# Moving the product with v beside the next tile's scores in a hand-planned attention and two-MLP kernel on one Trainium2 core

## Chip, cores and metric

One core of one Trainium2 chip. The metric is device time in microseconds (us) of one execution, from the launch of the program to its end; the kernel before takes 927.84 us (median of three runs).

## What is computed

Attention over 4 batches, 8 heads, 576 positions and head size 64, causal with a window of 128 and an ALiBi bias; then two MLPs over the resulting 2304 x 512 matrix. Cut to what matters:

```python
scores = scale * q @ k.T                     # per batch and head
scores = where(0 <= rel < 128, scores - slope * |rel|, -1e9)
attn = exp(scores - max) / (sum + 1e-9)
x = (attn @ v) as (2304, 512)
x = (silu(x @ w_gate) * (x @ w_val)) @ w_out        # d_ff 1536
out = silu(x @ w_in) @ w_out2                       # d_ff 2048
```

Everything is float32. Large products are made from a high and a low float32r part in three passes.

## The kernel before

The 2304 tokens are 18 tiles of 128 (tile 0 to tile 17), in three parts of six (`PT = 6`). Part by part the MLPs run over the 768 tokens of a part: `moe1` with 6 groups, `moe2` with 8. While they run over one part, the attention of the next part is worked in between, tile by tile. In this document part one is tiles 0 to 5, part two tiles 6 to 11, part three tiles 12 to 17.

No loop of the kernel runs in the order in which it is written. Every operation is handed to `plan.add` with an engine (or two to choose from), a cost in ns, a due time, the keys that it reads and writes, and the PSUM banks that it takes and gives back. `Plan.issue` (L95) then plays the engines forward: each time it takes the engine that can start earliest, and on it the operation that can start now and has the earliest due time (equal due times go in the order of `add`). The due time is no gate. An engine that has nothing else starts whatever is ready, so on the planner's idle engines (ScalarE, SyncE's DMA queue) things go as soon as they are ready; TensorE nearly always has a choice, and there the due time decides. The result is one fixed order for each engine; on the chip each engine works through its own order and waits on semaphores.

The eight PSUM banks are dealt out by the planner too (L341): at most 6 for the MLP products (`mm`), at most 6 for attention (`att`, of which 4 for scores `S`, 1 for the product with v `O`, 2 for turned probabilities `C`, 1 for transposes `T`), at most 4 for operand differences (`B`).

The attention of a tile i from tile 6 on (L1266 to L1278), both halves of four heads together:

- `load` (L406): k, q and v of the tile, by SyncE's queue (L425). v has a ring of three buffers, so the load of v for tile i + 3 has to wait for the products that read tile i.
- `prepare` (L433): TensorE transposes k (L445) and q (L453); copies and differences on ScalarE and VectorE.
- `score` (L473, matmuls L493): 24 matmuls in TensorE tiles of 64 x 128, four banks at once, due at(i).
- `attend` (L503): masks (L520) and bias (L527) on VectorE, exponent (L533) on ScalarE, normalisation on VectorE and GpSimd (L549, L550, L553), turning on TensorE (L570), copy to `u` on ScalarE, and two selections on GpSimd (L577 to `l`, L584 to `u`). They are due at(i), at(i + 1/4), at(i + 1/2) and at(i + 3/4). `u` has three buffers, `l` two.
- `weigh` (L590, matmuls L607): the product with v, 32 matmuls in TensorE tiles of 128 x 64, one bank, and one copy of 512 columns to `XST` (a `copy_op`, L348 on ScalarE). It was due at(i + 3/4), the time of the last turns of its own tile.

`at` is a line in each part: 33 us of due time a tile for tiles 6, 7, 8 and again for 9, 10, 11, with a leap between (at(9) is 132.96 us of due time after at(6)); about 39.1 us a tile in part three. Tiles 0 to 5 go by halves.

`operands` (L674) makes the Strassen operands of a part from `XST` or `ACC`, with up to four `B` banks. `out_sums` (L859) in part three loads kept output weights (`word`, `top`, L868), adds them (L357 on VectorE or L358 on GpSimd) and stores sums.

Of the kernel before, what the change touches and what calls it, by code (L numbers as in the profile page):

```python
# [201 lines left out]
def attention_moe_moe2_kernel(  # L202
# [40 lines left out]
    PT = NT // P // 3  # L243
    BT = PT // 2
    N = BT * P
    NP = H // 2
    G1, G2 = F1 // (2 * P), F2 // (2 * P)
    EARLY = 6
# [94 lines left out]
    def cost(kind, n):  # L343
        a, b = COST[kind]
        return a + b * n

    def copy_op(n, due, out, src, reads, writes, give=None, psum=True, slack=0.0):
        act = lambda: nc.scalar.activation(out(), src(), AF.Copy)  # L348
        dve = lambda: nc.vector.tensor_copy(out(), src())  # L349
        plan.add(  # L350
            "act", cost("act_ps" if psum else "act", n), due, act, reads, writes, give=give,
            other=[("dve", cost("dve", n), dve, not psum, 500.0)], slack=slack,
        )
# [46 lines left out]
    def first(i):  # L400
        return (i * P) % S == 0
# [4 lines left out]
    def load(i, nm, due):  # L406
        src, dst, slot = {
            "k": (k, KLD_R, i % 2),
            "q": (q, QLD_R, i % 2),
            "v": (v, VLD_R, i % 3),  # L410
        }[nm]
        t = dst[slot]
        step = H // 2 if i == 0 else H
        for h0 in range(0, H, step):
            for off, n, b, s in runs(i * P, P):
                o = t[off:off + n, h0:h0 + step]
                a = src[b, h0:h0 + step, s:s + n, :].rearrange("h s d -> s h d")
                keys = [
                    (nm, slot, hf, r)
                    for hf in range(2) if h0 <= 4 * hf < h0 + step  # L420
                    for r in range(2) if off <= 64 * r < off + n
                ]
                plan.add(
                    "sp", 1460.0 * step * n / (H * P), due,
                    lambda o=o, a=a: nc.sync.dma_start(out=o, in_=a),  # L425
                    writes=keys,
                )

    def loaded(i, nm, hf):
        slot = i % (3 if nm == "v" else 2)  # L430
        return [(nm, slot, hf, r) for r in range(2)]

    def prepare(i, hf, due):  # L433
        kn, qn = KLD_R[i % 2], QLD_R[i % 2]
        kr = KR[:, :, 2 * hf:2 * hf + 2, i % 2, :]
        bk, bq = Bank("T"), Bank("T")
        pk = lambda: bk.tile.rearrange("p (a b) -> p a b", b=P)
        pq = lambda: bq.tile.rearrange("p (a b) -> p a b", b=P)
        slot = (2 * i + hf) % len(QT_R)
        qt = QT_R[slot]  # L440

        def k_turn():
            for j in range(2):
                h = 4 * hf + 2 * j
                nc.tensor.transpose(pk()[:, j, :], kn[:, h:h + 2].rearrange("p h d -> p (h d)"), ident)  # L445

        def k_lo():
            nc.vector.tensor_tensor(kr[:, 1], pk()[:, 0:2], kr[:, 0].bitcast(F32), ALU.subtract)

        def q_turn():  # L450
            for j in range(2):
                h = 4 * hf + 2 * j
                nc.tensor.transpose(pq()[:, j, :], qn[:, h:h + 2].rearrange("p h d -> p (h d)"), ident)  # L453

        def q_hi():
            nc.scalar.activation(qt[:, 0], pq()[:, 0:2], AF.Copy, scale=-0.125)

        def q_lo():
            nc.vector.scalar_tensor_tensor(
                qt[:, 1], pq()[:, 0:2], -0.125, qt[:, 0].bitcast(F32), ALU.mult, ALU.subtract  # L460
            )

        kk, qk = ("KR", i % 2, hf), ("qt", slot)
        plan.add("pe", 2 * 109, due, k_turn, loaded(i, "k", hf) + ["ident"], [bk], take=bk)
        copy_op(256, due, lambda: kr[:, 0], lambda: pk()[:, 0:2], [bk], [kk])
        plan.add("dve", cost("dve", 256), due, k_lo, [bk, kk], [kk], give=bk)
        plan.add("pe", 2 * 109, due, q_turn, loaded(i, "q", hf) + ["ident"], [bq], take=bq)
        plan.add("act", cost("act_ps", 256), due, q_hi, [bq], [qk])
        plan.add("dve", cost("dve", 256), due, q_lo, [bq], [qk], give=bq)
# [120 lines left out]
    def weigh(i, halves, due):  # L590

        ob = Bank("O")
        ops = lambda hf: ob.tile.rearrange("p (a b) -> p a b", b=P)[:, 2 * hf:2 * hf + 2]
        parts, reads = {}, []
        for hf in halves:
            us, ls = (2 * i + hf) % len(U_R), (2 * i + hf) % len(L_R)
            parts[hf] = [(i, U_R[us])] if first(i) else [(i - 1, U_R[us]), (i, L_R[ls])]
            reads += [("uu", us)] + ([] if first(i) else [("l", ls)])
            reads += [x for tl, _ in parts[hf] for x in loaded(tl, "v", hf)]

        def product():
            for hf in halves:
                for p in range(2):
                    for a, (tl, m) in enumerate(parts[hf]):
                        for j in range(2):
                            l = 2 * p + j
                            nc.tensor.matmul(  # L607
                                ops(hf)[64 * j:64 * j + 64, p, :],
                                VLD_R[tl % len(VLD_R)][:, 4 * hf + l, :],
                                m[:, l, :],  # L610
                                start=(a == 0),
                                stop=(a == len(parts[hf]) - 1),
                            )

        plan.add("pe", 218 * len(halves) * (1 if first(i) else 2) + 290, due, product, reads, [ob], take=ob)
        ti = i % PT
        for n, hf in enumerate(halves):
            last = hf == halves[-1]
            xk = [("xt", ti, 2 * hf + p) for p in range(2)]
            if i >= PT:  # L620
                if last and len(halves) == 2:
                    all_k = [("xt", ti, c) for c in range(KC)]
                    copy_op(
                        512, due, lambda: XST[:, ti], lambda: ob.tile.rearrange("p (a b) -> p a b", b=P), [ob], all_k, give=ob
                    )
                elif len(halves) == 1:
                    copy_op(256, due, lambda: XST[:, ti, 2 * hf:2 * hf + 2], lambda: ops(hf), [ob], xk, give=ob)
                continue
            slot, t0 = x_slot(hf, ti // BT), (ti % BT) * P
            xh, xl = XOP[:, slot, 0, :, t0:t0 + P], XOP[:, slot, 1, :, t0:t0 + P]  # L630
            keys = [("X", slot, kk, ti % BT) for kk in range(2)]
            copy_op(256, due, lambda xh=xh, hf=hf: xh, lambda hf=hf: ops(hf), [ob], keys)
            plan.add(
                "dve", cost("dve", 256), due,
                lambda xl=xl, xh=xh, hf=hf: nc.vector.tensor_tensor(xl, ops(hf), xh.bitcast(F32), ALU.subtract),
                [ob] + [("ob", i, h) for h in halves[:n]], keys + [("ob", i, hf)], give=ob if last else None,
            )


    def x_slot(j, b):  # L640

        return ((0, 1), (2, 3))[j][b]
# [623 lines left out]
    def attention_part(part, at):  # L1266
        for i in range(part * PT, part * PT + PT):
            load(i, "k", at(i) - 14820.0)
            load(i, "q", at(i) - 20070.0)
            load(i, "v", at(i) - 7670.0)  # L1270
            for halves in [(0,), (1,)] if i < EARLY else [(0, 1)]:
                t0 = at(i + 0.5 * halves[0])
                for hf in halves:
                    prepare(i, hf, t0 - 8000.0)
                banks = score(i, halves, t0)
                for hf in halves:
                    attend(i, hf, [at(i + p / NP) for p in (2 * hf, 2 * hf + 1)], banks[hf])
                weigh(i, halves, at(i + 0.5 * halves[-1] + 1 / NP))  # L1278

    def ramp(x):  # L1280
        return 5000.0 + 6130.0 * min(x, 1) + 10170.0 * min(max(x - 1, 0), 1) + 7700.0 * max(x - 2, 0)
# [93 lines left out]
    def spread(part, t0, span):  # L1375
        attention_part(part, lambda x: t0 + (x - part * PT) / PT * span)

    attention_part(0, ramp)
    moe1_plain([0])
    t_next = state["t"] + 6000.0  # L1380
# [4 lines left out]
    t_moe2 = t_next - 6000.0 + (G1 - GP) * 22 * pe_cost(6, N) + (GP - 1) * 24 * pe_cost(6, N)  # L1385
    early = lambda x: t_next + 0.0 + (x - PT) * 33000.0
    attention_part(1, lambda x: early(x) if x < PT + PT // 2 else t_moe2 + 20000.0 + (x - PT - PT // 2) * 33000.0)
    moe1(0, range(GP, G1), "raw", True)
    flush()
# [52 lines left out]
```

## Time and profile before

| what | us |
| --- | --- |
| median of 3 runs | 927.84 (926.32 to 929.77) |
| the profiled execution | 929.85 |
| its span, first to last instruction | 928.1 |
| TensorE busy in the span | 907.4 (98%), 5758 matmuls |
| VectorE, ScalarE, GpSimd busy | 670.2, 531.3, 539.6 |

Read the engine shares first, then the stretches: the attention of parts two and three lies between about 114 and 640 us. In the timeline a row is one run of like instructions: start, duration, engine, line, what is written and read, the TensorE tile, the shape and the count; in square brackets how long the engine sat idle before it and who ended that. Durations of matmuls overlap, so the distance from start to start tells what one costs.

### The profile page before, as it was taken

How to read it: one execution, taken by the hardware profiler on the slowest of the kernel's cores; microseconds unless marked ns; L12 is line 12 of the kernel's file. 1: busy time of each engine (PE TensorE's matmuls, PEld its weight loads, DVE VectorE, ACT ScalarE, POOL GpSimd, SP SyncE). 2: the span in 40 equal slices, each digit the busy share in tenths (PEclk: the TensorE clock that was granted, in tenths of full speed). 3: DMA queues.
4: the chain of work that ended last, by engine and by line, in shares of the span. 5: the costliest groups of instructions: out<-in, count | busy, mean ns of one | idle time of the engine just before them, and what ended most of it. 6: DMA issues, size and time to landing. Idle time of an engine off the chain costs nothing.

```text
span 928.1 us, 17773 instructions
## 1 busy us (share of the span) xinstructions
PE 907.4 (98%) x5758; PEld 844.4 (91%) x5758; DVE 670.2 (72%) x1554; ACT 531.3 (57%) x1361; POOL 539.6 (58%) x628
## 2 busy tenths in 40 slices
PE   7999999999999999999999999999999999999998
PEld 5889899998987888999999889889899999999997
DVE  7888869889979788747576877676734666736663
ACT  6887567667967685754343575544354333474531
POOL 2766377787546669674331555464333335788566
PEclk9999999999999999999999999999999999999999
DMA  9988896898888987999877787978898888587702
GB/s 225 271 238 275 253 331 208 286 322 286 267 263 273 292 298 264 346 317 302 273 259 236 253 280 263 334 278 288 292 307 251 252 252 251 187 257 247 220 24 91
DMA packets 181676, 241.57 MB, mean 260 GB/s; under 512 B 68048, under 2 KB 97232, under 8 KB 181584
## 3 DMA queue, kind: packets, MB, share of 16 engines
q1 hardware_dynamic: 181584, 240.44, 79.8%
q8 instruction: 46, 0.75, 0.3%
q14 instruction: 46, 0.38, 0.1%
HBM read 169.61 MB, written 70.78 MB: 259 GB/s over the span
## 4 chain that ended last, share of the span: by engine, by line
PE 78%; DVE 10%; DMA 5%; POOL 2%; ACT 2%; issue 2%; SPq 0%; DVEq 0%; ACTq 0%; POOLq 0%
PE bank L905 15%; PE bank L906 14%; PE bank L907 14%; PE bank L1234 5%; PE bank L1236 4%; PE bank L1235 4%; PE bank L493 3%; PE bank L607 3%; PE bank L1201 3%; PE bank L1203 3%; PE bank L1202 3%; DMA raw<-in_moe_w_in_dram 2%; DVE word L758 2%; PE bank L1132 2%; PE bank L1131 2%
## 5 line engine op out<-in xcount | busy, mean ns | idle before, releaser
L905 PE MATMUL bank<-XOP,wu 128*128 128x384 f32 (+1 forms) x868 | 296.7, 342 | 6.9 <-DVE tmp L349 1.9
L906 PE MATMUL bank<-XOP,wu 128*128 128x384 f32 (+1 forms) x868 | 289.3, 333 | 1.7 <-DVE XOP L357 1.0
L907 PE MATMUL bank<-XOP,wu 128*128 128x384 f32 (+1 forms) x868 | 288.9, 333 | 0.0
L905 PEld LDWEIGHTS bank<-XOP,wu 128*128 128x128 f32 x868 | 163.1, 188 | 16.8 <-ACT tmp L348 3.3
L906 PEld LDWEIGHTS bank<-XOP,wu 128*128 128x128 f32 x868 | 163.4, 188 | 4.5 <-DVE XOP L357 2.4
L907 PEld LDWEIGHTS bank<-XOP,wu 128*128 128x128 f32 x868 | 163.1, 188 | 0.1
L348 ACT ACTIVATE tmp<-bank 128x384 f32<-128x384 f32 x133 | 62.2, 489 | 67.7 <-PE bank L907 45.3
L358 POOL TENSOR_TENSOR h<-tmp,h 128x384 fp32r<-128x384 f32 x55 | 56.6, 1037 | 72.2 <-ACT h L348 72.1
L1234 PE MATMUL bank<-wo,h 128*128 128x512 f32 (+1 forms) x218 | 87.2, 400 | 0.1
L1236 PE MATMUL bank<-wo,h 128*128 128x512 f32 (+1 forms) x218 | 85.6, 393 | 0.0
L1235 PE MATMUL bank<-wo,h 128*128 128x512 f32 (+1 forms) x218 | 85.6, 392 | 0.0
L1246 DVE TENSOR_TENSOR ACC<-bank,ACC 128x512 f32<-128x512 f32 (+1 forms) x97 | 64.2, 679 | 21.6 <-PE bank L1236 15.5
L951 DVE TENSOR_TENSOR bank<-bank,tmp 128x384 f32<-128x384 f32 x93 | 52.3, 562 | 32.9 <-PE bank L907 27.9
L358 POOL TENSOR_TENSOR wu<-word,wu 128x256 fp32r<-128x256 f32 x63 | 50.1, 809 | 44.5 <-ACT wu L348 39.3
L553 POOL TENSOR_TENSOR cs<-cs,st 128x512 f32<-128x512 f32 x36 | 39.5, 1097 | 62.5 <-DVE st L550 45.8
L1201 PE MATMUL bank<-h,wo 128*128 128x384 f32 (+1 forms) x216 | 72.9, 338 | 0.1
L1203 PE MATMUL bank<-h,wo 128*128 128x384 f32 (+1 forms) x216 | 71.4, 331 | 0.0
L1202 PE MATMUL bank<-h,wo 128*128 128x384 f32 (+1 forms) x216 | 71.4, 330 | 0.0
L758 DVE SCALAR_TENSOR_TENSOR word<-raw,top 128x512 int32<-128x512 int32 x68 | 59.2, 871 | 11.0 <-ACT top L755 9.0
L533 ACT ACTIVATE cs<-cs,st 128x128 f32<-128x128 f32 x144 | 56.2, 394 | 15.0 <-DVE st L527 14.8
L755 ACT ACTIVATE top<-raw 128x512 f16<-128x512 bf16 x68 | 53.7, 790 | 17.9 <-DMA raw<-in_moe_w_in_dram 6.4
L358 POOL TENSOR_TENSOR wu<-sums,wu 128x256 fp32r<-128x256 f32 x78 | 61.5, 818 | 0.9 <-ACT wu L348 0.9
(417 smaller groups left out, 2116.5 us busy)
## 6 DMA issues: line engine op xcount, KB each, us to landing
wu<-kept_i SPq DMA_DIRECT2D x112, 256.0 KB, 3.4
wu<-kept_g SPq DMA_DIRECT2D x72, 256.0 KB, 4.2
wu<-kept_v SPq DMA_DIRECT2D x72, 256.0 KB, 4.1
wo<-kept_o SPq DMA_DIRECT2D x34, 512.0 KB, 4.5
raw<-in_moe_w_out_dram SPq DMA_DIRECT2D x28, 512.0 KB, 4.7
kept_o<-wo SPq DMA_DIRECT2D x28, 512.0 KB, 4.2
kept_i<-wu SPq DMA_DIRECT2D x56, 256.0 KB, 3.3
kept_s<-later_raw SPq DMA_DIRECT2D x44, 256.0 KB, 4.4
```

Source lines behind the costliest of these rows:

```text
L358: pool = lambda: nc.gpsimd.tensor_tensor(out(), x(), y(), op)
L758: lambda: nc.vector.scalar_tensor_tensor(w.bitcast(I32), word, 13, top, ALU.logical_shift_right, ALU.bitwise_or),
L905: nc.tensor.matmul(ps, wh, xh, start=start, stop=False, skip_group_check=True)
L906: nc.tensor.matmul(ps, wh, xl, start=False, stop=False, skip_group_check=True)
L907: nc.tensor.matmul(ps, wl, xh, start=False, stop=stop, skip_group_check=True)
L1201: nc.tensor.matmul(ps[:, 0:n], wh, h[:, 0], start=(i == 0), stop=False)
L1202: nc.tensor.matmul(ps[:, 0:n], wh, h[:, 1], start=False, stop=False)
L1203: nc.tensor.matmul(ps[:, 0:n], wl, h[:, 0], start=False, stop=(i == 1))
L1234: nc.tensor.matmul(ps, hh, wh, start=(i == 0), stop=False)
L1235: nc.tensor.matmul(ps, hh, wl, start=False, stop=False)
L1236: nc.tensor.matmul(ps, hl, wh, start=False, stop=(i == 1))
L1246: plan.add("dve", cost("dve", n), due, lambda: nc.vector.tensor_tensor(acc, pv(), acc, ALU.add), [b], keys, give=b)
```

## The change

`weigh` of a tile from tile 6 on, if it isn't the last of its part, is due at(i + 1) in place of at(i + 3/4). at(i + 1) is also the due time of the scores of tile i + 1. Nothing else changes: no operation is added or left out. `EARLY` is 6, so this meets tiles 6 to 10 and 12 to 16; tiles 11 and 17 keep their due time, and so do tiles 0 to 5.

```diff
@@ -1275,7 +1275,8 @@
                 banks = score(i, halves, t0)
                 for hf in halves:
                     attend(i, hf, [at(i + p / NP) for p in (2 * hf, 2 * hf + 1)], banks[hf])
-                weigh(i, halves, at(i + 0.5 * halves[-1] + 1 / NP))
+                paired = i >= EARLY and i + 1 < part * PT + PT
+                weigh(i, halves, at(i + 1) if paired else at(i + 0.5 * halves[-1] + 1 / NP))
```

## Rows read from the trace of the kernel before

**Rows 1.** The page: busy time of each engine, share of the span, instructions

```profile
PE 907.4 (98%) x5758; PEld 844.4 (91%) x5758; DVE 670.2 (72%) x1554; ACT 531.3 (57%) x1361; POOL 539.6 (58%) x628
```

**Rows 2.** A stretch: length, busy time by engine, granted clock, DMA share, GB/s

```profile
114.00:640.00 526.00, 518.45 (x3210) 477.56 (x3212) 406.88 (x922) 325.95 (x838) 318.06 (x390) 1.00 0.85 284
```

**Rows 3.** PE timeline: moved products with v of tiles 9 and 16, scores after

```profile
270.10 1.09 PE L607 MATMUL bank<-u,vld 128*64 128x128 f32 x16
...
280.23 1.68 PE L493 MATMUL bank<-KR,qts 64*128 64x256 f32 x24
...
593.68 0.44 PE L607 MATMUL bank<-u,vld 128*64 128x128 f32 x4
...
595.02 0.44 PE L607 MATMUL bank<-u,vld 128*64 128x128 f32 x4 [0.24 <-POOL u L584]
...
603.88 1.64 PE L493 MATMUL bank<-KR,qts 64*128 64x256 f32 x24
```

**Rows 4.** PE timeline: scores of tile 8 in the main stream

```profile
160.95 0.34 PE L907 MATMUL bank<-XOP,wu 128*128 128x384 f32 x1
161.22 1.63 PE L493 MATMUL bank<-KR,qts 64*128 64x256 f32 x24
```

**Rows 5.** PE timeline: tile 7's product with v, its end and the passes after

```profile
163.50 0.44 PE L607 MATMUL bank<-u,vld 128*64 128x128 f32 x4
...
165.08 0.39 PE L607 MATMUL bank<-l,vld 128*64 128x128 f32 x4
165.40 0.45 PE L905 MATMUL bank<-XOP,wu 128*128 128x384 f32 x1
165.68 0.34 PE L906 MATMUL bank<-XOP,wu 128*128 128x384 f32 x1
165.86 0.33 PE L907 MATMUL bank<-XOP,wu 128*128 128x384 f32 x1
```

**Rows 6.** PE timeline, part one: scores right behind a product with v

```profile
33.00 0.39 PE L607 MATMUL bank<-u,vld 128*64 128x128 f32 x4
33.22 0.39 PE L607 MATMUL bank<-l,vld 128*64 128x128 f32 x4
33.53 0.97 PE L493 MATMUL bank<-KR,qts 64*128 64x256 f32 x12
```

**Rows 7.** PE timeline: end of tile 10's product with v, transposes behind it

```profile
313.36 0.39 PE L607 MATMUL bank<-l,vld 128*64 128x128 f32 x4
313.68 0.44 PE L445 MATMUL bank<-ident,klds 128*128 128x128 f32 x2
```

**Rows 8.** PE timeline: tile 6's product with v, scores of tile 7

```profile
117.06 0.44 PE L607 MATMUL bank<-u,vld 128*64 128x128 f32 x4
...
137.53 1.65 PE L493 MATMUL bank<-KR,qts 64*128 64x256 f32 x24
```

**Rows 9.** PE, DVE and SP timelines: a stall between tile 12's product and tile 13's scores

```profile
410.75 0.44 PE L607 MATMUL bank<-u,vld 128*64 128x128 f32 x4
...
417.34 0.44 PE L905 MATMUL bank<-XOP,wu 128*128 128x384 f32 x1 [0.64 <-ACT tmp L348]
...
415.20 0.69 DVE L357 TENSOR_TENSOR word<-word,top 128x512 f32<-128x512 f32 x1 [3.47 <-DMA wu<-kept_g]
...
407.56 0.32 SPq L868 DMA_DIRECT2D word<-kept_o  x1
```

**Rows 10.** Transfers that write word, 404 to 418 us: issue to landing

```profile
DMA to landing us min/median/max: 7.5/7.5/7.5
```

**Rows 11.** SyncE's queue waiting for the product with v: us in total, times, longest

```profile
SPq L425 <- PE bank L607: 13.6, 5, 4.6
```

**Rows 12.** DVE timeline: a mask behind the scores of tile 15

```profile
511.59 0.43 DVE L520 COPY_PREDICATED bank<-m_up,bank 128x256 f32<-128x256 uint8 x1 [1.93 <-PE bank L493]
```

**Rows 13.** PE timeline: the longest stall after the scores of tile 10

```profile
291.02 0.44 PE L905 MATMUL bank<-XOP,wu 128*128 128x384 f32 x1 [1.93 <-DVE tmp L349]
```

**Rows 14.** DVE timeline: a transfer awaited behind tile 14's product with v

```profile
503.25 0.69 DVE L357 TENSOR_TENSOR word<-word,top 128x512 f32<-128x512 f32 x1 [2.27 <-DMA top<-kept_o]
```

## Prediction

> **What bounds the kernel now.** The page's busy shares come first: TensorE is busy for 98% of the span, VectorE for 72% and the others for less than 60% [rows 1]. So the end is set by how much TensorE has to do and by how long it stands. The change touches only tiles 6 to 16, so I next cut out the stretch from 114 to 640 us: TensorE is busy for 518.45 of 526.00 us at a granted clock of 1.00 [rows 2], its upper level of 2.4 GHz. The clock has nothing to give back, and the whole visible idle time there is 526.00 - 518.45 = 7.55 us. No change of order in this stretch can win more than that 7.55 us and what TensorE loses inside its busy time when it passes from one kind of matmul to another. The timeline, read from start to start, shows those losses; it is the third view. The fourth is the queues of VectorE and SyncE at the places where TensorE stands.
>
> **What moves.** Nothing is added or removed. Ten products with v (tiles 6 to 10, 12 to 16) get a later due time, 8.25 us of due time for tiles 6, 7, 9 and 10, a quarter of 39.1, or 9.8, for 12 to 16, and 42 for tile 8, whose next tile starts after the leap in `at`. On TensorE the due time decides, so each product should be issued where the scores of the next tile are issued now, and just ahead of them, as it was added first. For tile 9 that is from 270.10 to about 280, for tile 16 from 593.68 to about 603 [rows 3]; these and tiles 10, 12, 13, 14 and 15 make seven that I expect to pair, with distances of about 8 to 11 us. The MLP stream between the two places comes 1.9 us earlier (one product takes 165.40 - 163.50 us [rows 5]), and from the scores on everything stands where it stood. So the sum has small terms only.
>
> **Passing from one kind of matmul to another.** Passes of the main stream start 0.18 us apart (165.68, 165.86) [rows 5], matmuls of the product 0.22 us a group of four (33.00, 33.22) [rows 6].
> - Into the scores from the main stream: 161.22 - 160.95 = 0.27, so 0.09 over [rows 4].
> - Out of the product: 165.40 - 165.08 = 0.32, so 0.10 over; then the first pass takes 165.68 - 165.40 = 0.28, again 0.10 over [rows 5].
> - From the product straight into scores: part one has it, 33.53 - 33.22 = 0.31, so 0.09 over [rows 6].
>
> A pair therefore keeps the last of these and loses the exit of the product (0.10 + 0.10) while the entry into the scores is the one it keeps: 0.20 saved. That holds for tile 9. For the other six, transposes stand right behind the product now, at 0.32 in place of 0.22 [rows 7]; they share its way back to the main stream, and will have a slow first pass of their own afterwards. There only the one boundary of 0.10 goes. Sum: 0.20 + 6 x 0.10 = 0.8 us saved. Bounds: nothing, if no pair forms, and 10 x 0.20 = 2.0 us, if all do and the transposes find other company.
>
> The Trainium skill ("TensorEngine Tiling (Array Packing)", Tiling Modes, Key Properties) says that a change of the tiling mode drains TensorE. It speaks against part of the gain, as the product (128 x 64) and the scores (64 x 128) are different modes and a pair still changes in between; the 0.09 of rows 6 agrees. By that rule alone a pair saves one change of four, 7 x 0.1 = 0.7 us, about the same as the sum has.
>
> Why seven and not ten: the scores take four banks at once, and behind a product that has just taken one they need a fifth. One row speaks for five being there: tile 7's product ran 2.3 us after the scores of tile 8 [rows 4, 5], with one group of passes between. That tile is as good as adjacent now, and waits for its own inputs; I expect no change. Tile 6's scores come 20.5 us after its product [rows 8], twice the distance of the others for 8.25 us of due time: they were held by banks (operand differences take up to four there), not by the due time, so the product will go before them, not with them. Tile 8's product lands in the scores of tile 9, where the first output products of a new MLP stage run beside its input products; I count no pair.
>
> **The wait of tile 16's product.** It stood 0.24 us for the last selection on GpSimd [rows 3]. Some 10 us later its inputs are long there: 0.2 us saved.
>
> **The stall behind tile 12.** Between the old place (410.75) and the scores of tile 13, TensorE stands for 0.64 us at 417.34, for a copy that hangs on VectorE; VectorE had stood for 3.47 us at 415.20 for a loaded `word` [rows 9]. That load was issued at 407.56 [rows 9] and took 7.5 us [rows 10], so it lands at 415.06, and it was issued ahead of the product that moves. With the product gone from 410.75, TensorE reaches the same place 1.9 us earlier and stands 1.9 us longer: the time that the product used to cover is lost here. That is the upper end, +1.9. The lower end is -0.6: with the product moved the planner may put VectorE's addition for the main stream ahead of the sum of `word`, and the stall goes. The order of two operations decides it; the transfer speaks for the upper end, the planner's freedom for the lower. I take +0.6, near the middle, and keep both ends.
>
> **What else is moved, and costed at nothing.** Each moved product draws a copy to `XST` behind it on ScalarE, busy for 326 of 526 us [rows 2]; if it held up main-stream copies by its 0.6 us or so each time and TensorE waited, the seven would cost about 4 us. The load of v three tiles on goes out when the product is done. SyncE's queue stands for it now, 13.6 us in five waits, the longest 4.6 [rows 11], with the weight loads queued behind; these waits move to the scores, and the v is wanted more than a tile later. VectorE's masks now wait for the scores by up to 1.93 us [rows 12] with the main-stream evacuations queued behind. The planner counts a product at 1.16 us (4 x 218 + 290 ns) while it takes 1.9, so each pair can make this wait 0.74 longer, 7 x 0.74 = 5.2 us if all of it reached TensorE. I take zero, since none of it does behind the row of 511.59: TensorE runs its queue on. `u` and `l` are held some 10 us longer, but the next tile writes its first `l` only after its scores.
>
> **The sum.** -0.8 - 0.2 + 0.6 = -0.4 us. The profiled execution took 929.85 us (928.1 span and 1.75 around it), 2.0 above the median; by the sum it becomes 929.4, and the median 927.84 becomes 927.4. A measurement of this kernel can tell about 0.5% (4.64 us) from no change: below 923.2 is faster, above 932.5 slower. My forecast is no change.
>
> **Rivals.**
> - *No pairs* (the change does not do what it says): the product goes first, takes a bank, and the scores wait for their four until the copy to `XST` is done, with main-stream passes between. Then nothing is saved at the boundaries, and the stall costs its upper end: -0.2 + 1.9 = +1.7, 929.5. For it: four banks at once, six for the main stream. Against: the fifth bank of rows 4 and 5.
> - *Slower*: the early main stream runs into transfers that have their own time. In each gap between old and new place it comes 1.9 us early, and where VectorE's queue stands for a load the 1.9 is lost, as behind tile 12. It decides from four of the seven gaps on: 4 x 1.9 - 1.0 = +6.6, 934.4. For it: DMA is busy 85% of the stretch [rows 2]. Against: I find only one further gap with such a wait, 2.27 us at 503.25, now covered by tile 14's product [rows 14].
> - *Faster*: the new order dissolves the stalls behind the scores, of which the longest is 1.93 us [rows 13], as VectorE catches up during a 3.5 us block in which TensorE asks it for nothing. To be seen it must take over half of the 7.55 us; at 5 us it gives -1.0 - 5 = -6, 921.8. Against: behind the scores everything stands where it stood.
>
> **How the numbers follow.** Forecast 0.66, no pairs 0.15, slower 0.09, faster 0.10. The unknown terms of the forecast (0 to 2.0 saved, -0.6 to +1.9, up to 4 or 5 us from ScalarE's copies or VectorE's waits, and some idle time re-dealt) put it between 922 and 931.5. The range from 922.0 to 931.5 holds it and the case without pairs and leaves out the two others, 0.19. Of the first two I give 0.02 to each side beyond 0.5%: faster 0.12, within 0.5% 0.77, slower 0.11.
>
> **What would show it.** Right: seven times a product (L607) directly followed by scores (L493) at 0.31 us for the step, no wait for `u` at tile 16, and TensorE's stall near 417 at 2.5 us or at none. Wrong: fewer pairs (banks), idle time of TensorE from 114 to 640 far from 7.55 us, or waits of VectorE for `word` in the other gaps.

## The result and the profile after

The changed kernel takes 932.49 us (median of 7 runs, 931.59 to 936.77) against 926.86 of the kernel before on the same chip: a ratio of 1.0064 (1.0046 to 1.0082), or 5.6 us slower. Two later comparisons gave 1.0039 (1.0024 to 1.0055) and 1.0058 (1.0034 to 1.0081); both stand below with the experiments. The time predicted was 927.4, no change; 932.5 lies just outside the range.

The page after (columns as in [rows 1]):

```profile
PE 904.1 (97%) x5758; PEld 842.7 (90%) x5758; DVE 674.6 (72%) x1557; ACT 530.1 (57%) x1363; POOL 539.7 (58%) x623
```

The work is the same, 5758 matmuls. So the next view is the stretch that answers to [rows 2], and the same cut at 264 us, behind the last tile that the prediction left without a pair (length, then busy time of PE, PEld, DVE, ACT, POOL, granted clock, DMA share, GB/s). After:

```profile
114.00:264.00 150.00, 143.98 (x907) 134.53 (x906) 129.70 (x280) 108.25 (x273) 99.87 (x117) 1.00 0.83 274
114.00:640.00 526.00, 514.15 (x3186) 474.90 (x3185) 408.87 (x921) 323.30 (x835) 314.17 (x380) 1.00 0.85 282
```

And the first part of it in the kernel before:

```profile
114.00:264.00 150.00, 147.24 (x922) 137.60 (x923) 129.75 (x281) 112.06 (x280) 108.29 (x129) 1.00 0.84 281
```

Over the whole stretch TensorE stands 526.00 - 514.15 = 11.85 us, 4.3 more than before, at a granted clock of 1.00 in both executions. From 114 to 264 us it is 150.00 - 143.98 = 6.02 against 2.76: 3.3 of the 4.3 us lie where the prediction costed the change at nothing. The rest, 5.83 against 4.79 us, is no more than this stretch varies by itself: two further executions of the changed kernel gave 4.49 and 5.36.

The start of a span differs by some 3 us from execution to execution: the first matmul of the main stream starts between 25.1 and 28.4 us in the sixteen profiles of this study. The granted clock sorts them. It starts between 25.1 and 26.1 us in the eight in which the clock stays at 1.00 until then, at 27.1 to 27.3 in the six in which it is 0.50 (1.2 GHz) for 3.4 us before that, and at 28.3 and 28.4 in the two in which it is 0.50 for 6.8 us. The profile of before is one of the six, that of after one of the eight (columns as above, before and after):

```profile
21.00:24.00 3.00, 3.00 (x23) 2.32 (x22) 2.15 (x5) 2.77 (x12) 2.81 (x5) 0.50 1.08 304
21.00:24.00 3.00, 3.00 (x40) 2.42 (x40) 2.12 (x9) 3.00 (x12) 2.93 (x5) 1.00 1.02 288
```

So I measure from the scores of tile 6, ahead of which nothing was changed, to the last matmul. Before, TensorE timeline (start, duration):

```profile
74.41 1.65 PE L493 MATMUL bank<-KR,qts 64*128 64x256 f32 x24
...
924.46 0.28 PE L1236 MATMUL bank<-wo,h 128*128 128x256 f32 x1
```

After:

```profile
72.47 1.65 PE L493 MATMUL bank<-KR,qts 64*128 64x256 f32 x24
...
926.84 0.28 PE L1236 MATMUL bank<-wo,h 128*128 128x256 f32 x1
```

That is 850.3 us before and 854.7 after: 4.3 us, as much as the idle time grew. In these two executions TensorE does the same work in the same busy time; it stands longer. Over all runs the clock has a part as well: the mean granted clock of the changed kernel is 0.996, 0.997 and 0.996 in its three comparisons, that of before 0.999 and 0.998 in the two later ones. The section on the stall near 231 us shows where it falls.

**The pairs are there.** The timeline of TensorE after, at tiles 9, 12 and 16:

```profile
280.46 0.40 PE L1236 MATMUL bank<-wo,h 128*128 128x512 f32 x1
280.79 1.09 PE L607 MATMUL bank<-u,vld 128*64 128x128 f32 x16
281.81 1.68 PE L493 MATMUL bank<-KR,qts 64*128 64x256 f32 x24
...
422.02 0.39 PE L607 MATMUL bank<-l,vld 128*64 128x128 f32 x4
422.34 1.68 PE L493 MATMUL bank<-KR,qts 64*128 64x256 f32 x24
...
605.56 0.39 PE L607 MATMUL bank<-l,vld 128*64 128x128 f32 x4
605.88 1.63 PE L493 MATMUL bank<-KR,qts 64*128 64x256 f32 x24
```

Seven products stand right ahead of the scores of the next tile (9, 10, 12 to 16), the step between them 0.32 us, and there is no wait for `u` left at tile 16 and none at all near 417 us. The other three, first row of each product and of the scores of the tile after it:

```profile
121.62 0.44 PE L607 MATMUL bank<-u,vld 128*64 128x128 f32 x4
...
135.20 1.65 PE L493 MATMUL bank<-KR,qts 64*128 64x256 f32 x24
159.43 1.65 PE L493 MATMUL bank<-KR,qts 64*128 64x256 f32 x24
...
162.78 0.44 PE L607 MATMUL bank<-u,vld 128*64 128x128 f32 x4
...
208.66 0.44 PE L607 MATMUL bank<-u,vld 128*64 128x128 f32 x4
...
246.49 1.56 PE L493 MATMUL bank<-KR,qts 64*128 64x128 f32 x24
```

Tile 6's product stands 14 us ahead of the scores of tile 7, tile 7's behind the scores of tile 8, tile 8's 38 us ahead of the scores of tile 9: no pair, as forecast. But tile 6's moved: counted from the scores of tile 6 it starts at 49.2 us in place of 42.7 [rows 8], and tile 8's product at 136.2 in place of 124.8. Tile 8's product before:

```profile
199.25 0.44 PE L607 MATMUL bank<-u,vld 128*64 128x128 f32 x4
```

**The new stalls.** The two longest of TensorE from 114 to 264 us, where the kernel before has none over 1.3 us (its longest of the whole stretch is that of [rows 13], at 291 us). The longest of before there, then the two after:

```profile
223.51 0.41 PE L905 MATMUL bank<-XOP,wu 128*128 128x384 f32 x1 [1.28 <-ACT XOP L348]
...
154.69 0.44 PE L905 MATMUL bank<-XOP,wu 128*128 128x384 f32 x1 [1.65 <-DVE tmp L966]
...
231.10 0.44 PE L905 MATMUL bank<-XOP,wu 128*128 128x384 f32 x1 [2.52 <-ACT tmp L348]
```

They come back in the two other profiles of this kernel, at 1.63 and 2.50 us both times. They belong to its order, not to the execution.

### The profile page after: what moved, and what is told of

It reads as the page before. It is cut to its first block, busy times and chain, and to the rows that moved or that the text cites. A ratio compares the mean times of both kernels' runs of the same rounds, so it can differ in the third digit from the quotient of the medians.

```text
span 931.1 us, 17783 instructions
## 1 busy us (share of the span) xinstructions
PE 904.1 (97%) x5758; PEld 842.7 (90%) x5758; DVE 674.6 (72%) x1557; ACT 530.1 (57%) x1363; POOL 539.7 (58%) x623
## 4 chain that ended last, share of the span: by engine, by line
PE 58%; DVE 9%; DMA 7%; POOL 3%; ACT 2%; issue 2%; SPq 0%; DVEq 0%; ACTq 0%; POOLq 0%
PE bank L905 11%; PE bank L907 11%; PE bank L906 10%; PE bank L1234 5%; PE bank L1236 4%; PE bank L1235 4%; DMA raw<-in_moe_w_in_dram 3%; DVE word L758 2%; DMA top<-kept_o 2%; PE bank L607 2%; PE bank L1132 2%; PE bank L1131 2%; PE bank L1133 2%; PE bank L1201 1%; PE bank L1203 1%
## 5 line engine op out<-in xcount | busy, mean ns | idle before, releaser
L758 DVE SCALAR_TENSOR_TENSOR word<-raw,top 128x512 int32<-128x512 int32 x68 | 61.4, 904 | 14.6 <-ACT top L755 10.2
L951 DVE TENSOR_TENSOR bank<-bank,tmp 128x384 f32<-128x384 f32 x93 | 52.1, 560 | 27.3 <-PE bank L907 22.1
L358 POOL TENSOR_TENSOR wu<-sums,wu 128x256 fp32r<-128x256 f32 x79 | 64.5, 845 | 2.2 <-ACT wu L348 2.2
```

Of the source, the lines that this page charges most:

```text
L358: pool = lambda: nc.gpsimd.tensor_tensor(out(), x(), y(), op)
L758: lambda: nc.vector.scalar_tensor_tensor(w.bitcast(I32), word, 13, top, ALU.logical_shift_right, ALU.bitwise_or),
```

## The experiments

The letters in the quoted expectations name theories that are explained there; my own text calls them by what they say. At the start there were two: that the loss comes from the pairs (VectorE's masks wait longer for the scores, the main stream's evacuations behind them), or from the three products that do not pair, by a new order of everything behind tile 6. A third, theory C of the quotes, lets any new order cost or give a few us at no particular place. The results first, in one table: the ratio of each with its 95% interval, TensorE's idle time from 114 to 264 us, and the time from the scores of tile 6 to the last matmul, both of one profiled execution.

| products moved, or other edit | ratio | idle, us | to the end, us |
| --- | --- | --- | --- |
| none (before) | 1 | 2.76 | 850.3 |
| 9, 10, 12 to 16 | 0.9993 (0.9974 to 1.0012) | 3.44 | 850.0 |
| 12 to 16 | 0.9987 (0.9963 to 1.0011) | 3.40 | 848.5 |
| 12 to 16, again | 0.9998 (0.9982 to 1.0014) | 2.36 | 847.2 |
| 9, 10 | 1.0008 (0.9985 to 1.0030) | 1.93 | 851.4 |
| 6 | 1.003 (1.001 to 1.005) | 4.46 | 850.9 |
| 6, 7, 8 | 1.0073 (1.0048 to 1.0098) | 6.00 | 854.8 |
| all but 8 | 1.0012 (0.9999 to 1.0026) | 4.84 | 851.8 |
| all (after) | 1.0064, 1.0039, 1.0058 | 6.02, 5.88, 5.87 | 854.7, 852.7, 854.7 |
| all, one VectorE operation held back | 1.007 (1.0044 to 1.0096) | 6.76 | 855.0 |
| all, two held back | 1.0033 (1.0016 to 1.005) | 4.93 | 850.1 |
| none; 6 due 2 us later | 1.0077 (1.0058 to 1.0095) | 5.56 | 854.6 |
| none; tile 7's preparation 2 us later | 1.003 (1.0009 to 1.0051) | 4.02 | 851.8 |
| none; tile 7's preparation 2 us earlier | 1.0039 (1.0019 to 1.0058) | 3.20 | 850.9 |

The two kernels of the same edit (12 to 16) differ by 1.3 us in the last column, the three profiles of after by 2.0: a single row of that column counts from about 2 us on. Some of these executions hold stretches of 3.4 us at a granted clock of 0.50 behind the scores of tile 6: two with 6, 7, 8 moved, one each with 9, 10, in the second and third of after, with one operation held back and with tile 7's preparation 2 us later.

**Which products cost.** All these edits replace one line of the changed kernel.

Only tile 6's product moved:

```diff
-                paired = i >= EARLY and i + 1 < part * PT + PT
+                paired = i == 6
```

> Only tile 6's product with v is due at the next tile's scores; nothing forms a pair with scores. Theory A (the loss is what moving tile 6's product does to the order behind it, from 117 us on): 4 to 6 us slower than before, with TensorE's idle time from 114 to 240 us up by 3 us or more. Theory B (the loss is VectorE's masks, queued behind paired scores): within 1 us of before. Theory C (any re-dealing of the order costs or gives a few us, at no particular place): anything from 4 us faster to 4 us slower, with stalls at places other than in the changed kernel.

Measured: 930.50 us, before 927.67. Nothing pairs, and some 2.8 us are lost (0.9 to 4.6 by the interval): less than the 4 to 6 expected if this move were the whole cause, and the idle time up to 264 us grew by 1.7 us, not 3. The stall near 154 us is there with tile 6 alone, that near 231 is not. TensorE from 114 to 264 us in it, and that stall:

```profile
114.00:264.00 150.00, 145.54 (x911) 135.39 (x909) 130.40 (x286) 108.92 (x275) 101.74 (x120) 1.00 0.82 274
...
153.36 0.45 PE L905 MATMUL bank<-XOP,wu 128*128 128x384 f32 x1 [1.65 <-DVE tmp L966]
```

Only the seven that pair:

```diff
-                paired = i >= EARLY and i + 1 < part * PT + PT
+                paired = i >= 9 and i + 1 < part * PT + PT
```

> Tiles 9, 10 and 12 to 16 are moved, the seven that pair; tiles 6, 7 and 8 keep their due time, so the order up to 270 us is that of before. Theory A: 0 to 1.5 us faster than before (the seven boundaries, 0.8 to 1.4 us). Theory B: 4 to 6 us slower, with VectorE's wait for the scores at 13 us as in the changed kernel and TensorE's stalls close behind the scores. Theory C: -3 to +3 us.

Measured: 928.16 us, before 927.67: no difference. So the loss is not in the pairs. The waits of VectorE's masks for the scores from 114 to 642 us, in us, count and longest, in the kernel before:

```profile
DVE bank L520 <- PE bank L493: 3.5, 6, 1.9
```

in this kernel:

```profile
DVE bank L520 <- PE bank L493: 11.0, 7, 3.8
```

and in the changed one:

```profile
DVE bank L520 <- PE bank L493: 13.8, 8, 3.8
```

They have tripled with the seven pairs, and the kernel takes the same time: what VectorE loses there doesn't show in it.

Only part three:

```diff
-                paired = i >= EARLY and i + 1 < part * PT + PT
+                paired = i >= 2 * PT and i + 1 < part * PT + PT
```

> Only the five pairs of part three are moved. Theory A: about 1 us faster. Theory B: 3 to 4 us slower (five sevenths of the loss). Theory C: -3 to +3 us, not five sevenths of seven_pairs.

Measured: 927.00 us, before 927.67. Again, in a later comparison, to see whether five pairs without the others win anything:

> The five pairs of part three alone, once more with more rounds, to see whether pairs are worth something: by the boundaries 5 x 0.1 us and the wait for u 0.2 us, 0.7 us faster at least; with tile 12's stall gone as well 1.5 us faster. If VectorE's longer wait at the masks reaches TensorE: 1 us slower or more.

Measured: 927.02, before 927.34, ratio 0.9998. Five pairs win nothing that can be measured.

Only tiles 9 and 10:

```diff
-                paired = i >= EARLY and i + 1 < part * PT + PT
+                paired = 9 <= i < 11
```

> Only the two pairs of part two are moved. Theory A: within 0.5 us of before. Theory B: 1 to 2 us slower. Theory C: -3 to +3 us, and the sum with tiles_12_16 is not that of seven_pairs.

Measured: 927.94, before 927.67. No difference.

Only the three that do not pair:

```diff
-                paired = i >= EARLY and i + 1 < part * PT + PT
+                paired = 6 <= i < 9
```

> Only the three tiles whose products form no pair are moved. Theory A (the loss is theirs, through the order from 117 to 240 us): 5 to 6 us slower than before, all of the changed kernel's loss or a little more, since the pairs' gain is missing. Theory C (every re-dealing is its own draw): within 2.8 us (tile6_alone) plus or minus 2, no matter what the changed kernel does.

Measured: 934.59, before 927.70. This is the whole loss and more, without one pair. Moving tile 6's product changes the order on all engines from about 117 us on, and with it moved tile 8's changes it once more: the stall near 231 us is in this kernel (2.51 us) and not in that with tile 6 alone. No run moves tile 7's or tile 8's product alone, so what tile 8's costs without tile 6's is open.

All but tile 8:

```diff
-                paired = i >= EARLY and i + 1 < part * PT + PT
+                paired = i >= EARLY and i != 8 and i + 1 < part * PT + PT
```

> The change for all but tile 8. Theory A with tile 6 as its only root: 2 to 3 us slower than before (tile6_alone less the pairs' gain). If tile 8's product, which the order re-dealt by tile 6 puts 8 us later, is what raises the stall near 231 us: that stall is absent and the time is 2.5 us or more below changed_again. If the stall near 231 stays: tile 8 has no part in it.

Measured: 928.92, before 927.70, ratio 1.0012. The stall of 2.5 us near 231 us isn't there. The changed kernel itself, on the same chip:

> The changed kernel once more, on the chip and in the rounds of the three runs below, so that these can be set against it: 5 to 6 us slower than before, with TensorE standing for about 2.5 us near 231 us.

Measured: 931.36, before 927.70. So tile 8's product costs 2.4 us between these two, whose intervals overlap at their ends, and by the pair of tile 6 alone and tiles 6, 7, 8 (1.0073 - 1.003, on different chips) about 4. The terms add up: tile 6 about +2.8, tile 8 +2.4 to +4, the pairs between +0.7 and -1.7 us (1.0008 of two tiles; 1.0012 - 1.003 with and without pairs beside tile 6). The sum lies between 3.5 and 7.5 us; the changed kernel's three comparisons give 3.6 to 5.9.

**The stall near 231 us.** VectorE after, just ahead of it:

```profile
226.45 3.18 DVE L758 SCALAR_TENSOR_TENSOR word<-raw,top 128x512 int32<-128x512 int32 x1
229.55 0.55 DVE L695 TENSOR_TENSOR bank<-ACC 128x384 f32<-128x384 f32 x1
230.02 0.55 DVE L951 TENSOR_TENSOR bank<-bank,tmp 128x384 f32<-128x384 f32 x1
```

GpSimd and ScalarE after, in the same stretch:

```profile
226.24 2.15 POOL L358 TENSOR_TENSOR wu<-sums,wu 128x256 fp32r<-128x256 f32 x3
228.36 0.72 POOL L358 TENSOR_TENSOR wu<-word,wu 128x256 fp32r<-128x256 f32 x1
...
229.66 0.63 ACT L348 ACTIVATE wo<-word 128x512 fp32r<-128x512 f32 x1 [3.81 <-DVE word L758]
...
230.57 0.86 ACT L348 ACTIVATE tmp<-bank 128x384 f32<-128x384 f32 x2
```

L758 joins two halves of a loaded weight into `word`, in SBUF only. It takes 0.69 us as a rule (median of 48 in either kernel) and 3.18 here, and it ends 0.55 us after a row of four GpSimd instructions (226.24 to 229.08). Behind it in VectorE's queue is the main stream's addition L951, behind its reader in ScalarE's queue the copies to `tmp` that TensorE waits for. Two theories: the join is the trouble and is to be put elsewhere, or any VectorE operation with all its inputs in SBUF would stand there. For the first, the join and all that needs it are handed out only after the ScalarE copies:

```diff
+    def call(self, n, fn, held):
+        _, _, preds, take, give, _ = self.ops[n]
+        if n == 1664 or preds & held.keys():
...
+            held[n] = fn
+        else:
+            fn()
+        if n == 1535:
+            for f in held.values():
+                f()
+            held.clear()
...
-            fn()
+            self.call(n, fn, held)
```

> The changed kernel with one VectorE operation (the join of a weight's words, L758, which took 3.18 us at 226.45 beside GpSimd's run of sums) put three places later in VectorE's order, and the ScalarE copy that needs it with it; TensorE's and GpSimd's orders stay. Theory D (the new order has put an operation that cannot run beside GpSimd ahead of additions that TensorE waits for): TensorE's stall of 2.5 us near 231 goes to under 0.5 us and the time falls by 2 to 2.5 us against changed_again. Theory E (TensorE is held there by VectorE's whole load after the operands): the stall stays above 1.5 us or comes back within 10 us of it, and the time is that of changed_again within 1 us.

Measured: 933.72, before 927.70; this theory fell. The stall of 1.87 us is what VectorE's load as a whole was expected to leave, the time is not: it is 2.4 us above the changed kernel's 931.36 and not within 1. VectorE, GpSimd and TensorE of this run, a fence each:

```profile
230.34 2.91 DVE L695 TENSOR_TENSOR bank<-ACC 128x384 f32<-128x384 f32 x1
233.17 0.55 DVE L951 TENSOR_TENSOR bank<-bank,tmp 128x384 f32<-128x384 f32 x1
```

```profile
229.98 2.17 POOL L358 TENSOR_TENSOR wu<-sums,wu 128x256 fp32r<-128x256 f32 x3
232.09 0.74 POOL L358 TENSOR_TENSOR wu<-word,wu 128x256 fp32r<-128x256 f32 x1
```

```profile
234.22 0.44 PE L905 MATMUL bank<-XOP,wu 128*128 128x384 f32 x1 [1.87 <-ACT tmp L348]
```

The next operation, a difference of two `ACC`, 0.55 us long after, now takes 2.91 beside the same four, and the addition still stands behind it. So the second theory: hold both back, so that the addition comes ahead of both (`n in (1664, 1485)` in the third line of the diff), beside the changed kernel once more:

> As sum_held, but both VectorE operations that stand there with all inputs in SBUF (the join of words L758 and the difference of two ACC blocks L695) are put behind the one addition in PSUM (L951) that TensorE waits for, and the ScalarE copies that need them with them; TensorE's and GpSimd's orders stay. Theory F (whichever VectorE operation with only SBUF inputs comes first there waits until GpSimd's run of four sums is over, and with it all of VectorE's queue): the addition runs at once, TensorE's stall near 230 us falls from 2.5 us to under 0.5 us, the first of the two held operations takes the 2 to 3 us in its place, and the time is 1.5 to 2.5 us below changed_third. Theory E (VectorE's load as a whole): the stall stays above 1.5 us and the time within 1 us.

> The changed kernel in the rounds of the next run, as its measure: 0.4 to 0.65% slower than before, TensorE standing for 2.5 us near 230 us.

Measured: 930.28 with both held, 932.79 for the changed kernel, before 927.34. VectorE, GpSimd and TensorE with both held:

```profile
226.09 0.56 DVE L951 TENSOR_TENSOR bank<-bank,tmp 128x384 f32<-128x384 f32 x1 [0.56 <-PE bank L907]
226.56 2.07 DVE L758 SCALAR_TENSOR_TENSOR word<-raw,top 128x512 int32<-128x512 int32 x1
```

```profile
225.25 2.13 POOL L358 TENSOR_TENSOR wu<-sums,wu 128x256 fp32r<-128x256 f32 x3
227.35 0.73 POOL L358 TENSOR_TENSOR wu<-word,wu 128x256 fp32r<-128x256 f32 x1
```

```profile
229.73 0.44 PE L905 MATMUL bank<-XOP,wu 128*128 128x384 f32 x1 [1.08 <-ACT XOP L348]
```

The addition, which reads PSUM, runs in 0.56 us in the middle of the four; the join takes 2.07, again until they are done. TensorE's stall goes from 2.50 to 1.08, over the 0.5 that I expected, and what is left waits for the held difference. The time falls by 2.5 us, though the two intervals (1.0016 to 1.005 and 1.0034 to 1.0081) overlap. That settles the mechanism of this stall: here GpSimd's run holds off VectorE's operations on SBUF, and the queue behind them with it.

The 1.4 us by which the stall became shorter are not all of the 2.5. Five of the profiles have this stall at 1.9 to 2.5 us; in four of them, all but the first of after, the granted clock falls to 0.50 behind it for 3.4 us. TensorE in the second profile of the changed kernel, and a part of that stretch (columns as above):

```profile
229.72 0.44 PE L905 MATMUL bank<-XOP,wu 128*128 128x384 f32 x1 [2.50 <-ACT tmp L348]
...
231.42 0.53 PE L907 MATMUL bank<-XOP,wu 128*128 128x384 f32 x1
231.74 0.53 PE L905 MATMUL bank<-XOP,wu 128*128 128x384 f32 x1
...
231.10:234.40 3.30, 3.30 (x12) 3.21 (x12) 3.18 (x7) 2.51 (x7) 0.00 (x0) 0.50 1.07 414
```

Passes start 0.32 us apart there in place of 0.18 [rows 5]; ten of them make 10 x 0.14 = 1.4 us, an estimate. With both operations held back the profiled execution has no such stretch, and the mean granted clock of the runs is 0.999, for 0.996 of the changed kernel beside it. So where the clock falls, the stall seems to cost about 1.4 us more than it lasts; no run separates the two.

**Does it take a later product?** The kernel before, with tile 6's product due 2 us later, a quarter of the change's shift:

```diff
-                weigh(i, halves, at(i + 0.5 * halves[-1] + 1 / NP))
+                weigh(i, halves, at(i + 0.5 * halves[-1] + 1 / NP) + 2000.0 * (i == 6))
```

> The kernel before with one number changed: tile 6's product with v is due 2 us later than it was, in place of 8.25. Nothing pairs. Theory A' (a later product of tile 6 is bad in itself, by how late it is): a quarter of tile6_alone's loss, under 1 us. Theory C (any new order from 117 us on is a new draw of collisions): a change of its own size and sign, up to 4 us either way, with stalls at other places than in tile6_alone.

Measured: 934.47, before 927.34, ratio 1.0077. A quarter of the shift costs more than all of it: the loss doesn't grow with how late the product is. It is also more than the 4 us that I allowed for a new order. Then two edits that touch no product at all, the due time of tile 7's preparation (`t0` is at(7)):

```diff
-                    prepare(i, hf, t0 - 8000.0)
+                    prepare(i, hf, t0 - 8000.0 + 2000.0 * (i == 7))
```

> The kernel before, with one due time changed that has nothing to do with a product with v: the transposes and copies that prepare tile 7 are due 2 us later. The planner deals the order anew from that place on. Theory C (the order of before behind tile 6 is one of many, and a good one; any new order costs some us): TensorE idle for 4.5 to 6.8 us from 114 to 264 us, as in the kernels with tile 6's product moved, and a ratio of 1.003 to 1.008. Theory G (it takes a later product of tile 6): idle 1.9 to 3.5 us there, as in the kernels that leave that product, and a ratio within 0.002 of 1.

```diff
-                    prepare(i, hf, t0 - 8000.0)
+                    prepare(i, hf, t0 - 8000.0 - 2000.0 * (i == 7))
```

> As the run before, with the same work due 2 us earlier instead of later; another new order from that place on. Theory C: idle 4.5 to 6.8 us of TensorE from 114 to 264 us and a ratio of 1.003 to 1.008 here as well. Theory G: idle 1.9 to 3.5 us, ratio within 0.002 of 1. If the two runs differ, a new order is a draw that can go either way, and neither theory holds as put.

Measured: 930.54 and 931.43, before 927.65. Both lose about as much as tile 6 alone, one with work moved later and one with it moved earlier. By the ratios it takes no later product; a new order from there on is enough. Five dealt here (6; 6, 7, 8; 6 by 2 us; tile 7's preparation either way) are clearly not as good as that of before; a sixth, all but 8, loses 0.12%, which can't be told from nothing. But not any new order costs: the kernels with pairs alone are dealt anew from about 270 or 410 us on, and none of them loses. By the idle time I was wrong: 4.02 and 3.20 us lie below the 4.5 to 6.8 that I wrote, the second within what the order of before shows. Where the 3 us of these two kernels lie is open; their profiled executions took only 1.5 and 0.6 us more than before's from the scores of tile 6 to the end.

## Why the prediction was wrong

- **Seven pairs, not ten, and which:** right, tile by tile. The fifth bank of [rows 4, 5] was there each time. The reason for tile 8 was not: its product, expected in the scores of tile 9, came only 11.4 us later and stands 38 us ahead of them.
- **The boundaries, 0.8 us saved:** the sizes are right. Into tile 9's product 280.79 - 280.46 = 0.33, where passes of that stage start 0.23 apart, so 0.10 over; product to scores 0.32 for 0.31 forecast. As a gain it can't be told from nothing: 0.9993 for all seven. Tile 9's product is half as long as the 1.9 us that I took for each (16 matmuls, 1.09 us, in [rows 3]).
- **Tile 16's wait for `u`, 0.2:** gone.
- **The stall behind tile 12, +0.6 between -0.6 and +1.9:** the lower end came. No row of TensorE from 400 to 425 us has a wait, though not as I had put it: the sum of `word` went from VectorE to GpSimd, where it waits 2.84 us for its transfer with the main stream's additions on another queue. GpSimd after:

```profile
416.94 1.29 POOL L358 TENSOR_TENSOR word<-word,top 128x512 f32<-128x512 f32 x1 [2.84 <-DMA word<-kept_o]
```

- **VectorE's masks, 0 of at most 5.2:** the zero was right, the bound wrong. The waits grew by 7.5 us with the seven pairs and by 10.3 with all ten (3.5 to 13.8), more than 7 x 0.74; TensorE runs its queue on.
- **SyncE's queue behind the products, costed at nothing:** it waits 9.6 us in five waits, the longest 4.5, for the 13.6 and 4.6 of [rows 11]; nothing was lost there.
- **"From the scores on everything stands where it stood":** this is the step that failed, and with it the zero for tiles 6 and 8. I asked of each product whether it would pair, and took one that doesn't as one that costs nothing. But it is issued elsewhere all the same: tile 6's went 6.5 us later, tile 8's 11.4. The planner takes at each step what can start first, so one operation less at a place changes what is free for the next and, from there on, the whole order of five engines. I let that freedom in at one place only, the stall behind tile 12, where it was worth 2.5 us between its ends. It had a term of its own to get, "some idle time re-dealt", and I gave it a share of the range, not a price. By the runs it is +2.8 us for tile 6 and +2.4 to +4 for tile 8.
- **"The clock has nothing to give back":** true, but it had something to lose, and the sum has no term for that. Behind the new stall near 231 us it fell in four of five profiles, at about 1.4 us each by the estimate above.
- **The rivals:** none had it. The slower one reached 934.4 by VectorE's waits for loads in four gaps; the pairs that would have made them cost nothing. The faster one was the nearest in kind, a new order that dissolves stalls, and had the wrong sign: the order of before had few (2.76 us in 150), so a new one had more to lose than to win. The 7.55 us of idle time, which I read as the most that can be won, also said how little a new order could improve on.
- **The stall near 231 us**, with the clock behind it 2.5 of the 5 us: shown by the runs with operations held back. The one near 154 us is not: four VectorE operations on SBUF stand ahead of it beside GpSimd work, but I have not tried it. The remainder of the loss is spread over stalls of 0.3 to 0.5 us, and of it nothing is shown.

## What to carry to other kernels

In a kernel whose order a greedy planner deals, a changed due time isn't a local edit: find the first place where the order differs and take everything behind it as a new draw, to be priced by what the present order loses there. Where that is little (here 1 to 2% of TensorE's time), there is more to lose than to gain: from 117 us on six of seven draws lost, the changed kernel among them, and from 270 us on none lost or gained anything that shows. So give the edit only to the tiles where it does what it is for (here 9, 10, 12 to 16 lose nothing), and keep the early ones as they are. Ahead of a critical addition, look for a VectorE operation on SBUF that meets a run of GpSimd instructions. And look at the granted clock behind a new stall, in more than one profile.

## What the runs showed of the hardware

Near 231 us a VectorE operation with both inputs in SBUF that met GpSimd instructions on SBUF waited until the whole run of them was over: 3.18 us for 0.69 beside four, 2.91 for 0.55 and 2.07 for 0.69 beside the same four met earlier or later. An operation beside it that reads one input from PSUM took its usual 0.56. That is not the rule, though. VectorE and GpSimd of the same kernel elsewhere:

```profile
344.41 1.22 DVE L758 SCALAR_TENSOR_TENSOR word<-raw,top 128x512 int32<-128x512 int32 x1 [0.52 <-POOL wo L358]
344.34 3.75 POOL L358 TENSOR_TENSOR wu<-sums,wu 128x256 fp32r<-128x256 f32 x4
```

Here the join, 1.22 us long, is over at 345.63, with more than 2 us of the four still to come, and the four take 3.75 us, 0.9 more than near 231 (226.24 to 229.08): the join waited for the instruction under way alone, and then GpSimd waited for it, and once more for an addition of VectorE at 346.62. Of the 15 joins of the changed kernel that met one of GpSimd's additions with another close behind, 14 did so; only that at 226.45 waited for the whole run. What decides it is open. The Trainium skill ("SBUF — State Buffer", SBUF: two separate sides) names a cause, a port pair that the two engines share as an exclusive lock, held for the whole instruction. The rows at 344 us agree; those near 231 go beyond it, as VectorE did not get the pair between GpSimd instructions that follow each other. The planner (`port_free` in `Plan.issue`) reckons with a lock that is free after each instruction, which fits most joins and not this one.
